# Sums for the means of values in three rounds over three tiles, the means put two tiles ahead, and all later keys reordered by GpSimd

## The chip, the cores and the metric

The kernel runs on one NeuronCore of a Trainium2 chip. The metric is the device time of one execution in microseconds (us). Engines are named as in the profile: PE is TensorE (PEld its weight loads), DVE is VectorE, ACT is ScalarE, POOL is GpSimd, and SP is the engine that issues most DMAs.

## The reference

Attention over 4 batches, 8 heads, 768 tokens and 64 numbers a head, in which each token sees its neighbours within 16 positions and, besides, one summary of every block of 32 tokens: the maximum of the block's keys and the mean of its values. The result feeds a mixture of 8 experts with one expert a token.

```python
k_sum = k.reshape(B, H, nb, block, D).max(axis=3)
v_sum = v.reshape(B, H, nb, block, D).mean(axis=3)          # the means of values: 24 a batch and head
scores_s = scale * einsum('bhsd,bhnd->bhsn', q, k_sum) + log(block)
a = softmax(concat([where(|i - j| < 16, scale * q @ k.T, -1e9), scores_s]))
attn = a @ concat([v, v_sum])                               # x, the experts' input, is attn by token
e_idx = argmax(x @ w_gate)                                  # one expert a token
out[e_idx == e] = gate * sigmoid(x @ w_output_gate)[e] * (relu(x @ w1[e]) @ w2[e])
```

## The kernel before

**Attention** works on 24 tiles of 128 tokens, six a batch, in a loop (L552) whose pass i is called tile i below; tiles 6, 12 and 18 begin batches 1, 2 and 3. The order of all instructions in it is written by hand. Pass i does, in this order:

- `scores(i + 2)` on PE (`sp`, L321) and the mask on DVE (`pr`, L326);
- `values` and `norm` of the tiles that are due, from tile 4 on tile i - 1 (`pv`, L364; `den`, `xs`, L374 to L378);
- `turn_p(i)`: PE turns the probabilities (`pt`, L353), ACT evacuates them (`pT`);
- `smallest(i + 2)` on DVE (`mn`, L333), then `exps(i + 1)` on ACT (`pr`, L342);
- the lists `early` and `put`: `gather_means` and `put_means`;
- now and then a reorder of queries on POOL, and the lists `rts` (routing) and `todo` (`prep_q`, `prep_k`, `means`);
- `subtract(i + 2)` on POOL (`pr`, L338), the store of `xs`, V loads on SP (L585 to L591), and reorders of keys: for batch 1 on POOL, for batches 2 and 3 on ACT (`nat_k`, L234), three each;
- turns of `xs` for the routing (`xtr`, L390).

**Means.** The windows of V of a batch lie in `VW`, 12 blocks of 64 rows. `means(b)` (L249) multiplies them with constant matrices: 12 matmuls into four 32-row strips of one PSUM bank (`ms`, L253), a 13th for the last 16 tokens (L255), and an ACT evacuation into `MT`. They run in one piece: in tile 2 for batch 0, and in tiles 5, 11 and 17 for batches 1, 2 and 3. `gather_means(b)` (L259) adds the two halves of each mean by a matmul (`mg`, L261) and evacuates them into `mst`; it runs in tiles 2, 6, 12 and 18. `put_means(t)` (L267) copies the 24 means into both of tile t's windows in `VW`, one on ACT and one on DVE; it runs one pass before the tile's `values`, so in pass t from tile 4 on, and for tiles 0 to 3 two at a time in passes 2 and 3.

**PSUM.** Four tags of two banks each ("TR", "S", "PT", "PV") are handed out in turn by `bank` (L215), so that every eighth allocation meets the same bank.

**Experts.** At the end of tile 18 SP begins to load weights (`raw`, L801). Which expert's weights these are comes from small DVE steps on the routing counts (`early_slots`, the last of them `esia`, L667, in tile 18), and the token lists that POOL fetches (`lst`, L763) wait for the list scatters (`l_dr`, L472). ACT and DVE split each weight tile in two (L809, L810) between the passes 19 to 23. After the last tile the experts' matmuls (`hp` L839 to L841, `yp` L933 to L935) keep PE busy to the end.

Of the kernel before, what the change touches and what calls it, by code (L numbers as in the profile page):

```python
# [21 lines left out]
P = 128  # L22
# [50 lines left out]
def constants():  # L73
# [21 lines left out]
    for m in range(3):  # L95
        c[r, C_AVG + 32 * m + 2 * m + (r + PAD) // 32] = 1.0 / 32.0
    c[LW + NS:LW + NS + PAD, C_AVG + 96 + 6] = 1.0 / 32.0
    for j in range(NS):
        c[32 * (j // 6) + 1 + j % 6, C_SUM + j] = 1.0
        if j % 6 == 5 and j < NS - 1:  # L100
            c[32 * (j // 6 + 1), C_SUM + j] = 1.0
    return c
# [89 lines left out]
def attention(tc, const, sa, sb, st, ps, dr, q, k, v, id_sb, c_sb, wg_sb, x_dr, l_dr, rt, late_work):  # L192
# [55 lines left out]

    def means(b):  # L249
        mp = bank([P, H * D], f"ms{b}")  # L250
        for m in range(3):
            for j in range(4):
                nc.tensor.matmul(mp[32 * j:32 * j + 32], lhsT=c_sb[0:LW, C_AVG + 32 * m:C_AVG + 32 * m + 32],  # L253
                                 rhs=VW[b % 2][0:LW, 3 * j + m, :, 0:D], start=m == 0, stop=m == 2 and j < 3)
        nc.tensor.matmul(mp[96:P], lhsT=c_sb[0:W, C_AVG + 96:C_AVG + P], rhs=VW[b % 2][:, NB - 1, :, 0:D],  # L255
                         start=False, stop=True)
        evac(MT.rearrange("p h d -> p (h d)"), mp)

# [11 lines left out]

    ms, km = {}, {}

# [253 lines left out]
    def later(i, work, when=todo):  # L526
        when.setdefault(i, []).append(work)
# [24 lines left out]
    for i, (b, tok) in enumerate(tiles):  # L552
# [166 lines left out]
class Experts:  # L719
# [3 lines left out]
    def __init__(self, tc, const, ps, w1, w2, id_sb, x_dr, l_dr, rt, out):  # L723
        self.tc, self.const, self.ps, self.w1, self.w2 = tc, const, ps, w1, w2
        self.id_sb, self.x_dr, self.l_dr, self.rt, self.out = id_sb, x_dr, l_dr, rt, out
        self.slots, self.expert, self.raw, self.lists = {}, {}, {}, {}

    def fixed(self, pool, name, n, shape, dt):
# [292 lines left out]
```

## Time and profile before

| | us |
|---|---|
| median of 3 runs (lowest, highest) | 553.32 (552.46, 553.39) |
| the profiled execution | 555.07 |
| its span, first to last instruction | 553.3 |
| busy PE, DVE, ACT, POOL in the span | 490.2, 382.3, 328.8, 238.5 |
| attention, from the first `sp` to the last `pv` | 16.7 to 194.6 |
| experts' matmuls without a pause | 221 to 481 |

A row of the time line reads: start (us), duration (us), engine, line, operation, output<-inputs, shapes, how many instructions it merges (x), and in brackets how long the engine sat idle before it and what ended that. A row of the windows reads: stretch, its length, busy us (and instructions) of PE, PEld, DVE, ACT and POOL, the granted PE clock (1.00 is full), the DMA share, and GB/s. Many matmuls of a row are two instructions each, so `sp` of one tile shows as x32.

### The profile page before, as it was taken

Reading aid. Unit: us, or ns where it says so; the run is one execution under the profiler, and the core shown is the slowest. Engines: PE = TensorE matmul, PEld = TensorE weight load, DVE = VectorE, ACT = ScalarE, POOL = GpSimd, SP = SyncE. Lnnn points to the kernel's source line nnn. Section 1 sums busy time; section 2 is a strip of 40 time slices with the busy share of each in tenths; the row PEclk is TensorE's granted clock in tenths of the full one; section 3 lists DMA queues with packets and bytes.
Section 4 is the critical chain, followed back from the end, with each engine's and each line's share of the span. In section 5 each row is a group of like instructions: output and inputs, shape, how many; then the busy total and the mean of one; then the engine's idle time right before and its main releaser. Section 6 shows DMA issues by size and latency. Waiting matters only on the chain.

```text
span 553.3 us, 12768 instructions
## 1 busy us (share of the span) xinstructions
PE 490.2 (89%) x4396; PEld 413.4 (75%) x4396; DVE 382.3 (69%) x822; ACT 328.8 (59%) x634; POOL 238.5 (43%) x268
## 2 busy tenths in 40 slices
PE   6686999898984887999999999999999999968880
PEld 6545677577563776889898998989989898846660
DVE  3748579989979776866666665575765757648891
ACT  4455597697565754555555655465654656537780
POOL 8755426358585551387453363434411203121110
PEclk9898999999998697999999999999999999989996
DMA  9998947867246478386856759576694664648860
GB/s 235 198 243 189 251 117 190 197 127 155 67 81 189 135 199 276 42 275 218 292 193 217 234 165 289 175 262 170 233 322 142 242 231 153 210 145 309 291 239 20
DMA packets 105810, 109.53 MB, mean 198 GB/s; under 512 B 43294, under 2 KB 68030, under 8 KB 105728
## 3 DMA queue, kind: packets, MB, share of 16 engines
q1 hardware_dynamic: 96208, 88.20, 54.9%
q0 software_dynamic: 9520, 20.33, 12.1%
q8 instruction: 39, 0.64, 0.5%
q14 instruction: 43, 0.35, 0.2%
HBM read 97.53 MB, written 13.59 MB: 201 GB/s over the span
## 4 chain that ended last, share of the span: by engine, by line
PE 57%; issue 12%; DMA 10%; DVE 9%; ACT 7%; POOL 2%; POOLq 0%; SPq 0%; DVEq 0%; ACTq 0%
PE yp L934 7%; PE yp L935 7%; PE hp L839 7%; PE yp L933 7%; PE hp L840 7%; PE hp L841 7%; DMA out_dram<-y,lst 5%; DMA raw<-in_moe_w_dram 3%; PE sp L321 3%; PE pv L364 3%; PE ms L253 2%; PE pt L353 2%; DVE pr L326 2%; DMA xg<-x_dr,lst_half 2%; PE xp L821 1%
## 5 line engine op out<-in xcount | busy, mean ns | idle before, releaser
L839 PE MATMUL hp<-xhl,w1h 128*128 128x256 f32 x384 | 109.7, 288 | 3.4 <-DVE hl L843 3.4
L840 PE MATMUL hp<-xhl,w1h 128*128 128x256 f32 x384 | 109.7, 286 | 0.0
L841 PE MATMUL hp<-xhl,w1l 128*128 128x256 f32 x384 | 109.5, 286 | 0.0
L809 ACT ACTIVATE w2h<-raw 128x512 fp32r<-128x512 f32 x104 | 63.8, 629 | 70.1 <-PE yp L935 31.4
L810 DVE TENSOR_TENSOR w2l<-raw,w2h 128x512 fp32r<-128x512 f32 x104 | 69.8, 686 | 42.1 <-ACT w2h L809 41.4
L933 PE MATMUL yp<-w2h,hh 128*128 128x512 f32 x216 | 86.5, 400 | 1.2 <-ACT hh L903 1.2
L935 PE MATMUL yp<-w2h,hl 128*128 128x512 f32 x216 | 84.9, 394 | 0.2
L934 PE MATMUL yp<-w2l,hh 128*128 128x512 f32 x216 | 85.0, 394 | 0.0
L776 POOL DMA_INDIRECT xg<-x_dr,lst x28 | 33.1, 1182 | 112.6 <-PE xp L821 100.6
L839 PEld LDWEIGHTS hp<-xhl,w1h 128*128 128x128 f32 x384 | 74.4, 194 | 5.1 <-DVE hl L843 3.6
L840 PEld LDWEIGHTS hp<-xhl,w1h 128*128 128x128 f32 x384 | 74.7, 195 | 0.9
L841 PEld LDWEIGHTS hp<-xhl,w1l 128*128 128x128 f32 x384 | 74.7, 195 | 0.0
L810 DVE TENSOR_TENSOR w1l<-raw,w1h 128x512 fp32r<-128x512 f32 x104 | 67.6, 703 | 8.8 <-ACT w1h L809 7.7
L843 DVE SCALAR_TENSOR_TENSOR hl<-hp,hh 128x256 fp32r<-128x256 f32 x96 | 39.3, 420 | 43.4 <-ACT hh L842 43.3
L842 ACT ACTIVATE hh<-hp 128x256 fp32r<-128x256 f32 x96 | 36.2, 379 | 52.6 <-PE hp L841 50.5
L338 POOL TENSOR_TENSOR pr<-pr,mn 128x960 f32<-128x960 f32 x24 | 45.1, 1881 | 49.2 <-DVE mn L333 26.7
L809 ACT ACTIVATE w1h<-raw 128x512 fp32r<-128x512 f32 x104 | 57.5, 620 | 5.8 <-DMA raw<-in_moe_w_dram 4.8
L933 PEld LDWEIGHTS yp<-w2h,hh 128*128 128x128 f32 x216 | 40.7, 189 | 10.0 <-ACT hh L903 2.1
L935 PEld LDWEIGHTS yp<-w2h,hl 128*128 128x128 f32 x216 | 40.6, 188 | 9.8 <-DVE hl L904 1.1
L211 ACT ACTIVATE pT<-pt 120x512 f32<-120x512 f32 x48 | 26.2, 594 | 34.0 <-PE pt L353 34.0
L934 PEld LDWEIGHTS yp<-w2l,hh 128*128 128x128 f32 x216 | 40.7, 188 | 7.6
L763 POOL DMA_INDIRECT lst<-l_dr,rowib x34 | 36.8, 1082 | 18.8 <-issue 9.5
(303 smaller groups left out, 901.1 us busy)
## 6 DMA issues: line engine op xcount, KB each, us to landing
raw<-in_moe_w_dram SPq DMA_DIRECT2D x208, 256.0 KB, 5.1
raw_k<-in_k_dram SPq DMA_DIRECT2D x12, 512.0 KB, 6.5
raw_q<-in_q_dram SPq DMA_DIRECT2D x12, 512.0 KB, 5.9
x_dr<-xs POOLq DMA_DIRECT2D x24, 256.0 KB, 3.2
vw<-in_v_dram SPq DMA_DIRECT2D x44, 128.0 KB, 4.7
vw<-in_v_dram SPq DMA_DIRECT2D x33, 64.0 KB, 4.4
vw<-in_v_dram POOLq DMA_DIRECT2D x11, 64.0 KB, 6.0
lst<-l_dr,rowib POOLq DMA_INDIRECT x34, 3.8
```

Source lines behind the costliest of these rows:

```text
L338: nc.gpsimd.tensor_tensor(pr, pr, mns.pop(i).unsqueeze(2).to_broadcast([P, H, W]), ALU.subtract)
L763: i = nc.gpsimd.indirect_dma_start(out=lst[:, t, :], out_offset=None, in_=self.l_dr, in_offset=bass.IndirectOffsetOnAxis(ap=self.slots[s][ ...
L809: nc.scalar.activation(hi, raw, AF.Copy)
L810: nc.vector.tensor_tensor(lo, raw, hi.bitcast(F32), ALU.subtract)
L839: nc.tensor.matmul(hp, lhsT=w_h[:, fs], rhs=self.xh[:, c, :], start=c == 0, stop=False)
L840: nc.tensor.matmul(hp, lhsT=w_h[:, fs], rhs=self.xl[:, c, :], start=False, stop=False)
L841: nc.tensor.matmul(hp, lhsT=w_l[:, fs], rhs=self.xh[:, c, :], start=False, stop=c == NC - 1)
L842: nc.scalar.activation(hh[:, j, :], hp, AF.Relu)
L843: nc.vector.scalar_tensor_tensor(hl[:, j, :], hp, 0.0, hh[:, j, :].bitcast(F32), ALU.max, ALU.subtract)
L933: nc.tensor.matmul(y, lhsT=hh[:, j, tk], rhs=w_h, start=j == 0, stop=False)
L934: nc.tensor.matmul(y, lhsT=hh[:, j, tk], rhs=w_l, start=False, stop=False)
L935: nc.tensor.matmul(y, lhsT=hl[:, j, tk], rhs=w_h, start=False, stop=j == NF - 1)
```

## The change

Five things change, all in attention.

1. `means(b)` is cut in three rounds, `means(b, m)`. Round m sums blocks 4m to 4m + 3 (before, strip j took blocks 3j to 3j + 2, so that each round needed the whole batch; the constants follow). The rounds of batch 0 stand in tiles 0, 1 and 2, those of batches 1 to 3 in the three tiles that end with 5, 11 and 17. The gather stays where it was.
2. The sum keeps a bank of its own over the three tiles: "TR" shrinks to one bank, a tag "MS" gets one, and `bank` now turns over seven banks. `take_x` of the experts takes "TR" and "MS" in turn.
3. `put_means(t)` runs one pass earlier, but not before the batch's gather: in pass 2 for tiles 0 to 3, in pass t - 1 for most, and for the first two tiles of batches 1 to 3 together in passes 6, 12 and 18.
4. `smallest(i + 2)` moves behind `exps(i + 1)` and behind the lists `early` and `put`, so DVE puts means first and reduces afterwards.
5. The six reorders of keys of batches 2 and 3 move from ACT to POOL.

```diff
-PB = {"S": 2, "PT": 2, "PV": 2, "TR": 2}
+PB = {"S": 2, "PT": 2, "PV": 2, "TR": 1, "MS": 1}
...
-    turn = itertools.cycle(("TR", "S", "PT", "PV"))
+    turn = itertools.cycle(("TR", "S", "PT", "PV", "S", "PT", "PV"))
...
-    def means(b):
-        mp = bank([P, H * D], f"ms{b}")
-        for m in range(3):
-            for j in range(4):
-                nc.tensor.matmul(mp[32 * j:32 * j + 32], lhsT=c_sb[0:LW, C_AVG + 32 * m:C_AVG + 32 * m + 32],
-                                 rhs=VW[b % 2][0:LW, 3 * j + m, :, 0:D], start=m == 0, stop=m == 2 and j < 3)
+    def means(b, m):
+        if m == 0:
+            mps[b] = ps.tile([P, H * D], F32, name=f"ms{b}", tag="MS", bufs=PB["MS"])
+        mp = mps[b]
+        for j in range(4):
+            nc.tensor.matmul(mp[32 * j:32 * j + 32], lhsT=c_sb[0:LW, C_AVG + 32 * m:C_AVG + 32 * m + 32],
+                             rhs=VW[b % 2][0:LW, 4 * m + j, :, 0:D], start=m == 0, stop=m == 2 and j < 3)
...
-        later(first - (1 if b == 0 else 2), lambda b=b: means(b), early if b == 0 else todo)
+        for m in range(3):
+            later(first - (3 if b == 0 else 4) + m, lambda b=b, m=m: means(b, m), early if b == 0 and m == 2 else todo)
         later(first - 1, lambda b=b: gather_means(b), early)
     for t in range(n):
-        later(live[t] - 1, lambda t=t: put_means(*tiles[t]), put)
+        first = live[t - t % TB]
+        later(max(live[t] - 2, first - 1), lambda t=t: put_means(*tiles[t]), put)
...
         turn_p(i)
-        if i + AHEAD < n:
-            smallest(i + AHEAD)
         if i + 1 < n:
             exps(i + 1)
         for x in early.pop(i, []) + put.pop(i, []):
             x()
+        if i + AHEAD < n:
+            smallest(i + AHEAD)
...
-                reorder("k", kb, u, "p" if kb == 1 else "a")
+                reorder("k", kb, u, "p")
...
-    def take_x(self, n, tag="TR"):
+    def take_x(self, n):
...
+            tag = next(self.turn)
```

In the order of the instructions, names carry batch and tile: `ms1` is the sum of batch 1, `sp12` belongs to tile 2 of batch 1, and the last number of a name is a buffer's. PE at the end of tile 5, before:

```order
L279 MATMUL qtr111_925<-id_sb_66,nat_q11_810 128x128 x4
L253 MATMUL ms1_931<-vw1_170,c_sb_68 32x512 x12
L255 MATMUL ms1_931<-vw1_170,c_sb_68 32x512
L390 MATMUL xtr04_956<-id_sb_66,xs04_882 128x128 x4
L321 MATMUL sp120_963<-kt1_168,qt0_165 64x120
```

The whole sum stands there in a row, ahead of the next tile's scores. PE at the end of tile 3 now, ahead of the scores of tile 6 (`sp10`), the first of batch 1:

```order
L283 MATMUL ktr121_689<-id_sb_66,nat_k12_562 128x128 x4
L256 MATMUL ms1_697<-vw1_170,c_sb_68 32x512 x4
L394 MATMUL xtr00_715<-id_sb_66,xs00_603 128x128 x4
L394 MATMUL xtr01_722<-id_sb_66,xs01_628 128x128 x4
L325 MATMUL sp100_728<-kt1_168,qt1_166 64x120
```

Four of the twelve matmuls have moved up to here; four more stand at the end of tile 4, and the last four with the 13th where all thirteen were.

DVE in tile 18, where the means of batch 3 (`mst3`) arrive, before (`mn32` is the minimum of tile 20, `esa` to `esia` the expert's index for the first weights):

```order
L378 TENSOR_TENSOR xs25_2387<-pv251_2378,den25_2388 128x256
L333 TENSOR_REDUCE mn32_2407<-pr32_2366 128x8
L209 COPY vw1_170<-mst3_2412 24x8x64
L209 COPY lg2_2181<-lt23_2418 128x32
L657 TENSOR_REDUCE esa_2436<-pasta_2333 128x3
L659 TENSOR_SCALAR nonea_2439<-esa_2436 128x3
L660 TENSOR_TENSOR rowa_2343<-rowa_2343,nonea_2439 128x3
L661 TENSOR_SCALAR rowia_2347<-rowa_2343 128x3
L662 TENSOR_SCALAR rowia_2347<-rowa_2343 128x3
L667 TENSOR_SCALAR esia_2437<-esa_2436 128x3
```

And now:

```order
L382 TENSOR_TENSOR xs25_2387<-pv251_2378,den25_2388 128x256
L211 COPY vw1_170<-mst3_2410 24x8x64 x2
L337 TENSOR_REDUCE mn32_2416<-pr32_2366 128x8
L211 COPY lg2_2188<-lt23_2420 128x32
L663 TENSOR_REDUCE esa_2438<-pasta_2333 128x3
L665 TENSOR_SCALAR nonea_2441<-esa_2438 128x3
L666 TENSOR_TENSOR rowa_2343<-rowa_2343,nonea_2441 128x3
L667 TENSOR_SCALAR rowia_2347<-rowa_2343 128x3
L668 TENSOR_SCALAR rowia_2347<-rowa_2343 128x3
L673 TENSOR_SCALAR esia_2439<-esa_2438 128x3
```

The minimum has moved behind two copies that wait for the gather; what follows it keeps its place. POOL in tiles 5 and 6, now (`nat_k20` and `nat_k21` are the first keys of batch 2; before, their two rows were not there, and the others stood in the same order):

```order
L342 TENSOR_TENSOR pr11_872<-pr11_872,mn11_914 128x960
L387 DMA x_dr_74<-xs04_893 128x512
L238 COPY nat_k20_952<-raw_k20_713 128x1024
L238 COPY nat_q12_1033<-raw_q12_536 128x1024
L342 TENSOR_TENSOR pr12_981<-pr12_981,mn12_1031 128x960
L387 DMA x_dr_74<-xs05_1002 128x512
L238 COPY nat_k21_1064<-raw_k21_839 128x1024
```

One copy of keys is added behind each of three subtractions and their stores, ahead of the next query reorder or subtraction.

More of the change, by code (lines that the diff above doesn't have):

```diff
@@ L95, in constants @@
     for m in range(3):
[L96 to L101, printed above, removed]
+        c[r, C_AVG + 32 * m + 3 * m + (r + PAD) // 32] = 1.0 / 32.0
+    c[LW + NS:LW + NS + PAD, C_AVG + 96 + 9] = 1.0 / 32.0
+    for blk in range(NB):
+        at = 32 * (blk % 4) + 3 * (blk // 4)
+        c[at + 1, C_SUM + 2 * blk] = c[at + 2, C_SUM + 2 * blk + 1] = 1.0
+        if blk:
+            c[at, C_SUM + 2 * blk - 1] = 1.0
+    c[96 + 9, C_SUM + NS - 1] = 1.0
     return c
@@ L247, in load_vw @@
                 (engine or nc.sync).dma_start(t[p0:p0 + m, :, 0:D], v[b, :, s0 + r0:s0 + r0 + m, :].rearrange("h s d -> s h d"))
[L249 to L257 removed]
+    def means(b, m):
[5 more added lines that the diff above has]
+                             rhs=VW[b % 2][0:LW, 4 * m + j, :, 0:D], start=m == 0, stop=m == 2 and j < 3)
+        if m == 2:
+            nc.tensor.matmul(mp[96:P], lhsT=c_sb[0:W, C_AVG + 96:C_AVG + P], rhs=VW[b % 2][:, NB - 1, :, 0:D],
+                             start=False, stop=True)
+            evac(MT.rearrange("p h d -> p (h d)"), mp)
     def gather_means(b):
@@ L726, in __init__ @@
         self.slots, self.expert, self.raw, self.lists = {}, {}, {}, {}
+        self.turn = itertools.cycle(("TR", "MS"))
     def fixed(self, pool, name, n, shape, dt):
```

2 lines of the change are left out of this document (1 added, 1 removed).

## The prediction

> **What bounds the kernel now.** I read the windows first, to see which engine is full in which stage.
>
> ```profile
> 65.00:78.00 13.00, 13.00 (x192) 8.15 (x190) 6.89 (x15) 9.83 (x19) 5.75 (x5) 1.00 0.77 210
> 91.00:104.00 13.00, 9.72 (x176) 8.03 (x176) 12.38 (x29) 7.70 (x15) 6.78 (x8) 1.00 0.89 217
> 234.00:247.00 13.00, 13.00 (x88) 11.92 (x87) 8.56 (x23) 8.18 (x18) 9.74 (x8) 1.00 0.74 232
> ```
>
> The limit changes from tile to tile. Tiles 5 and 6 (65 to 78) fill PE; tiles 9 and 10 (91 to 104), where DVE does the routing as well, fill DVE with 12.38 of 13 us and leave PE 3.3 us idle. From 221 on the experts fill PE without a pause, and nothing of that stage is edited. So the change is worth what it takes off the way to the first expert's matmuls. The chain of waits tells what that way is at its end.
>
> ```profile
> 160.09 5.86 DMA raw<-in_moe_w_dram
> ...
> 198.09 12.49 DMA raw<-in_moe_w_dram
> ...
> 212.49 0.58 PE hp L839
> ```
>
> The weight stream starts at 160 and paces the rest, but it starts only when DVE has computed the expert's index in tile 18. So attention up to tile 18 is on the path, and a shift there reaches the end.
>
> **Tiles 2 to 4: the means of batch 0 and the copies of means.** First the time line of DVE, of POOL and of ACT.
>
> ```profile
> 38.20 3.15 DVE L209 COPY vw<-mst 24x512 f32<-24x512 f32 x2 [4.56 <-ACT mst L211]
> 47.33 2.35 DVE L209 COPY vw<-mst 24x512 f32<-24x512 f32 x2
> 49.71 2.48 DVE L293 TENSOR_REDUCE km<-ktr 128x16 f32<-128x512 f32 x4
> 93.10 0.42 DVE L209 COPY vw<-mst 24x512 f32<-24x512 f32 x1
> ```
>
> ```profile
> 38.10 1.04 POOL L236 COPY nat_q<-raw_q 128x1024 f32<-128x1024 f32 x1 [4.43 <-DMA raw_q<-in_q_dram]
> 39.11 1.96 POOL L338 TENSOR_TENSOR pr<-pr,mn 128x960 f32<-128x960 f32 x1
> 47.45 1.95 POOL L338 TENSOR_TENSOR pr<-pr,mn 128x960 f32<-128x960 f32 x1 [4.22 <-DVE mn L333]
> 51.66 1.53 POOL L300 COPY kt<-km 128x288 f32<-128x288 f32 x4 [2.26 <-DVE km L293]
> ```
>
> ```profile
> 47.45 2.33 ACT L211 ACTIVATE kt<-ktr 128x384 f32<-128x384 f32 x8
> ```
>
> A copy of means takes 0.42 us alone, but two of them took 3.15 and 2.35 us, and they ended (41.35, 49.68) with the POOL work that ran beside them (41.07, 49.40): DVE stood until POOL was through. DVE has no pause from 38.20 to 52.2, then `k_sum` (L300) follows, and it releases the scores of batch 1. After the change the copies stand ahead of the minimum, so the subtraction can't be running beside them. The gather also comes earlier; here is PE.
>
> ```profile
> 32.05 2.78 PE L253 MATMUL ms<-vw,c_sb 64*32 64x512 f32 x24
> 34.76 1.04 PE L255 MATMUL ms<-vw,c_sb 120*32 120x512 f32 x2
> 52.14 1.88 PE L321 MATMUL sp<-kt,qt 64*64 64x120 f32 x32 [4.14 <-POOL kt L300]
> 53.94 3.73 PE L364 MATMUL pv<-vw,pT 120*64 120x65 f32 x64
> 60.34 1.05 PE L321 MATMUL sp<-kt,qt 64*64 64x120 f32 x32
> 61.32 1.15 PE L364 MATMUL pv<-vw,pT 120*64 120x65 f32 x32
> ```
>
> A sum costs 2.71 + 0.99 = 3.7 us of PE (from start to start), a round 2.71 / 3 = 0.9. With two rounds gone to tiles 0 and 1, where PE waits anyway, 1.9 us is left in tile 2 and the gather comes 1.8 us sooner, or less if the last V blocks land late; I take 1.5. On DVE, four copies in tile 2 and one in tile 3 cost 5 x 0.42 = 2.1 in place of 5.5. That makes 1.5 + 3.4 = 4.9 for DVE alone. But the maxima (`km`) are released by ACT's evacuations (`kt`, 47.45 to 49.78), and ACT wins less: about 2.2 through PE (the 1.5 of the gather, and `values` that no longer wait for the 3.15 us), and 0.6 for one copy fewer in tile 3, so 2.8. Term 1: **-3.0** (bounds -1.5 and -4.9).
>
> **The PE clock in tile 4.** While PE waits 4.14 us for the keys of batch 1, its clock falls: `sp` takes 1.88 in place of 1.05 and two tiles of `pv` 3.73 in place of 2 x 1.15, 2.26 us too much on a PE that is then the bound (with the turns behind it, 2.4). Here are the windows there and behind another pause, and the rows of two shorter pauses.
>
> ```profile
> 51.00:54.00 3.00, 1.86 (x34) 1.47 (x34) 1.19 (x2) 0.00 (x0) 2.34 (x6) 0.51 0.58 128
> 171.00:174.00 3.00, 3.00 (x47) 2.58 (x40) 2.88 (x8) 0.92 (x2) 1.13 (x2) 0.51 0.44 158
> ```
>
> ```profile
> 93.81 1.13 PE L321 MATMUL sp<-kt,qt 64*64 64x120 f32 x32 [1.30 <-ACT qt L211]
> 169.44 0.68 PE L390 MATMUL xtr<-id_sb,xs 128*128 128x128 f32 x4 [3.11 <-DVE xs L378]
> ```
>
> After the change a round of 0.9 stands in this pause, PE's `xtr` come about 2.2 sooner and the keys 3.0: the pause is 4.14 - 0.9 - (3.0 - 2.2), about 2.5 us. The clock fell after 3.11 us and not after 1.30; 2.5 lies between and nearer to 3.11. Both ends stay in the range, 0 and -2.4. I take full clock, but barely: 3.11 is a pause in which almost nothing ran, while the round cuts this one's idle in two. Term 2: **-2.4**.
>
> [...]
>
> **Batch 1, tiles 3 to 8.** Of its sum, round 0 falls into the pause above, round 1 costs 0.9 in tile 4, and tile 5, where PE is full, loses 1.8: net -0.9. From tile 6 ACT is nearly as full as PE. It loses three reorders, but gets the second copy of the first two tiles, and the wait of the gather still runs through it; that gives back about 0.6.
>
> ```profile
> L234 ACT ACTIVATE nat_k<-raw_k 128x1024 f32<-128x1024 f32 x7 | 7.4, 1061 | 0.1
> L236 POOL COPY nat_k<-raw_k 128x1024 f32<-128x1024 f32 x4 | 4.3, 1086 | 2.3 <-DMA raw_k<-in_k_dram 2.2
> ```
>
> A reorder takes the same on both engines. POOL is busy 5.75 of 13 us in tiles 5 and 6, and the copy stands behind the subtraction and the store, with a pass to spare before PE turns the keys; what it is moved past is the list scatters and the next query reorder, which have as much slack. I cost it at nothing; without that cover it is 1.06 us a copy. Term 3: **-0.3** (bounds +0.6 and -1.8).
>
> **Batches 2 and 3, tiles 9 to 18.** PE loses 1.8 us in tile 11 and in tile 17 and gets 0.9 in tiles 9, 10, 15 and 16, where it waits (1.30 us in tile 9). But there DVE is the bound, and it loses a cover:
>
> ```profile
> 93.79 1.45 DVE L425 TENSOR_TENSOR d<-lg,mx 128x48 f32<-128x48 f32 x1
> ```
>
> ```profile
> 93.25 1.92 POOL L338 TENSOR_TENSOR pr<-pr,mn 128x960 f32<-128x960 f32 x1 [1.40 <-ACT ls L211]
> 155.12 1.80 POOL L338 TENSOR_TENSOR pr<-pr,mn 128x960 f32<-128x960 f32 x1
> 169.86 1.00 POOL L763 DMA_INDIRECT lst<-l_dr,rowia  x1 [4.94 <-DMA l_dr<-pair,posi]
> ```
>
> The routing step at 93.79 stood behind the subtraction, and the 0.42 us copy before it (93.10) lay in that shadow. Now the copy comes ahead of the minimum: +0.42 in each of tiles 9, 10, 15 and 16. In tile 18 it matters most:
>
> ```profile
> 153.71 1.14 DVE L333 TENSOR_REDUCE mn<-pr 128x8 f32<-128x960 f32 x1
> 155.24 1.97 DVE L209 COPY vw<-mst 24x512 f32<-24x512 f32 x1 [0.38 <-ACT mst L211]
> 158.22 0.16 DVE L667 TENSOR_SCALAR esia<-esa 128x3 int32<-128x3 f32 x1
> ```
>
> Before, the minimum was done at 154.85 and the copy waited out the subtraction, until 157.2; `esia` followed at 158.2. Now the minimum waits for the gather and two copies. With the gather 1.7 sooner (153.5, after PE's 1.8), the copies end about 155.3 beside a query reorder, the minimum 156.45, the subtraction 158.4; then the small steps behind it, stalled as at 93.79, bring `esia` to about 159.1. So the weight index comes 0.8 later against the DVE of its batch, and the three scatters behind that subtraction, for which the token lists wait (169.86), 1.5. Against that, batch 2 wins about 1.1 by tile 14, its own two copies taken off, since tile 12 waits less for tile 11's sum. Sum: -1.1 for batch 2, +0.84 for the copies of tiles 15 and 16, +1.2 (between 0.8 and 1.5) for tile 18, near +1.0. Term 4: **+1.0** (bounds -1.5 and +2.5).
>
> **Tiles 21 to 23.** Putting two tiles ahead takes a wait away here:
>
> ```profile
> 178.00 1.00 ACT L342 ACTIVATE pr<-pr 128x960 f32<-128x960 f32 x1 [2.59 <-POOL pr L338]
> ```
>
> ```profile
> 179.69 0.51 PE L364 MATMUL pv<-vw,pT 120*64 120x65 f32 x10 [3.81 <-ACT vw L211]
> ```
>
> `values` of tile 21 waited for a copy queued on ACT behind the exponentials at 178.00. It now runs before them; the turn behind it, which had to wait until 179.69 + 1.1 = 180.8, starts when the exponentials end, at about 179.0. ACT's own queue hides part of that. Term 5: **-1.0** (bounds 0 and -3, the latter if the clock stays up there too).
>
> The bank turn is shorter by one, so that a query turn meets the bank of the scores of the same tile one allocation sooner; DVE has evacuated them by then in all but the routing tiles. I cost it inside term 4. The experts' `take_x` has two banks as before.
>
> **Sum.** -3.0 - 2.4 - 0.3 + 1.0 - 1.0 = -5.7 us on the profiled execution of 555.07 us:
>
> ```profile
> core 0: 553.3 us, clock 0.959
> ```
>
> The span is 553.3, and 1.8 us lie around it. The median of the runs is 553.32; the shift carries over to it: 553.3 - 5.7 = **547.6 us**. A measurement of this kernel can tell some 0.2%, 1.1 us, from no change.
>
> **Rivals.**
>
> *A, the clock still falls in tile 4.* For it: the pause of 3.11 us. Against it: the pause is cut by a round. Term 2 is then gone: 547.6 + 2.4 = **550.0 us**. Chance 0.30.
>
> *B, slower: the minimum behind the gather becomes the bound in tiles 6, 12 and 18.* In tile 18 the subtraction ran from 155.12; behind the gather (155.2 on the old times), two copies, and the minimum it would run from 157.4, 2.3 us later. It decides once the subtraction ends later than ACT is ready for the exponentials of that tile, one pass on. If no slack were left, three tiles at 2.3 us each cost 6.9: 547.6 + 6.9 = **554.5 us**. Against it: a pass lasts 5 us or more, and ACT's queue is full in tiles 7 and 13. Chance 0.09.
>
> *C, POOL's six copies of keys block DVE.* A POOL copy of queries runs 1.04 us at 38.10 beside a stalled DVE copy. If each new copy meets such a DVE step, 6 x 1.09 = 6.5 us are lost: 547.6 + 6.5 = **554.1 us**. Against it: in tiles 5 to 8, 12 and 13 DVE's only such steps are the copies of means; the 24 minima, the longest DVE steps there, are all but constant whatever POOL does:
>
> ```profile
> L333 DVE TENSOR_REDUCE mn<-pr 128x8 f32<-128x960 f32 x24 | 27.5, 1145 | 0.2
> ```
>
> Their mean of 1145 ns is that of the single one at 153.71. Chance 0.07.
>
> [...]
>
> **How the numbers follow.** Forecast 0.50, A 0.30, B 0.09, C 0.07; 0.04 are left for what I don't see. Each of B and C may come in part: about half of their chance ends below 552.2 still. Faster by over 0.2%: 0.50 + 0.30 + 0.05 = 0.85. Within 0.2%: 0.07. Slower: 0.08. The range goes from 543.4 (terms 1, 3 and 5 each at the better half of their bounds: 0.9 + 0.8 + 1.0, and 1.5 of term 4) to 552.2 (A, with term 1 at its low bound and 0.7 of term 4): 543.4 to 552.2.
>
> **What would show it.** In the profile after: the DVE copies of means at 0.42 us apiece in tile 2; `sp` of tile 6 about 3 us sooner than 52.14 and 1.05 us long (1.88 by A); tile 5's `ms` 1.9 us; the first weight load about 5 us sooner than 160; `hp` without a pause from about 215. Term 1 is wrong if a round of `ms` waits for V; B shows as ACT's exponentials waiting for POOL in tiles 7, 13 and 19; C as DVE copies that end with `nat_k`. If the weight stream starts 5 us sooner and the experts don't, the path was not what I take it for.

## The result, and the profile after

The changed kernel takes 555.65 us (median of 20 runs, 552.12 to 559.91) where the kernel before took 553.83 beside it: a ratio of 1.006, with a 95% interval of 1.0038 to 1.0082. It is slower by 0.6%. The ratio and its interval, here and below, compare executions of the two kernels that were not in a slower state of the chip, so it is not the quotient of the two medians (1.003). The forecast was 547.6, and the range ended at 552.2. The profiled execution has a span of 555.2 us at a mean granted clock of 0.945 (before: 553.3 and 0.959).

I read the profile after in the order of the prediction's steps. First the windows that stood at its head.

```profile
65.00:78.00 13.00, 13.00 (x194) 9.03 (x187) 7.86 (x21) 9.34 (x19) 6.83 (x7) 1.00 0.82 198
91.00:104.00 13.00, 11.29 (x182) 8.21 (x182) 12.44 (x31) 5.63 (x12) 5.66 (x5) 0.87 0.96 221
234.00:247.00 13.00, 13.00 (x101) 12.60 (x100) 8.45 (x32) 5.32 (x13) 7.17 (x7) 1.00 0.39 130
```

The limits are the same ones: PE in tiles 5 and 6 and in the experts, DVE (12.44 of 13) in tiles 9 and 10. New is the clock of 0.87 in the second row. Next PE in tiles 0 to 4.

```profile
24.85 1.09 PE L357 MATMUL pt<-id_sb,pr 128*120 128x128 f32 x8 [2.60 <-ACT pr L346]
25.88 1.86 PE L256 MATMUL ms<-vw,c_sb 64*32 64x512 f32 x8
27.67 1.88 PE L325 MATMUL sp<-kt,qt 64*64 64x120 f32 x32
...
52.29 1.54 PE L325 MATMUL sp<-kt,qt 64*64 64x120 f32 x32 [0.99 <-POOL kt L304]
53.77 2.09 PE L368 MATMUL pv<-vw,pT 120*64 120x65 f32 x64
```

Two things happen at once. The pause ahead of tile 6's scores is 0.99 us in place of 4.14 and the clock stays up there, as forecast. But the clock falls elsewhere (0.50 from 26.0 to 32.8 us): after a pause of 2.60 us, in which PE waits for tile 0's exponentials, the first round of the sum takes 1.86 us in place of the 1.06 that later rounds take, the scores 1.88 in place of 1.05. Tile 2's exponentials start 8.17 us behind tile 0's (31.97 and 23.80), where it was 5.65 before (28.43 and 22.78): 2.5 us lost. This profile also begins 1.0 us later, with tile 0's exponentials at 23.80 in place of 22.78. So tile 6's scores start at 52.29, where they started at 52.14. (`sp` takes 1.54 us there although the granted clock is 1.00 from 52 to 54 us; the forecast for full clock was 1.05.) Now DVE in tiles 2 and 18.

```profile
40.41 1.42 DVE L211 COPY vw<-mst 24x512 f32<-24x512 f32 x4 [4.04 <-ACT mst L213]
...
153.40 1.62 DVE L211 COPY vw<-mst 24x512 f32<-24x512 f32 x2 [0.37 <-ACT mst L213]
155.04 1.15 DVE L337 TENSOR_REDUCE mn<-pr 128x8 f32<-128x960 f32 x1
156.41 1.75 DVE L665 TENSOR_SCALAR nonea<-esa 128x3 f32<-128x3 f32 x1
...
158.53 0.16 DVE L673 TENSOR_SCALAR esia<-esa 128x3 int32<-128x3 f32 x1
```

Four copies in tile 2 take 1.42 us, with GpSimd idle beside them (0.00 us busy from 40 to 42 us). In tile 18 the minimum stands behind the copies, and a step of the index (`nonea`) ends at 158.16, with the subtraction beside it (156.34 to 158.12). GpSimd shows what follows.

```profile
156.34 1.78 POOL L342 TENSOR_TENSOR pr<-pr,mn 128x960 f32<-128x960 f32 x1 [1.95 <-DVE lg L211]
...
161.55 1.06 POOL L476 DMA_INDIRECT l_dr<-pair,posi  x1 [0.19 <-issue]
...
172.49 1.00 POOL L770 DMA_INDIRECT lst<-l_dr,rowia  x1 [6.62 <-DMA l_dr<-pair,posi]
...
178.37 1.00 POOL L783 DMA_INDIRECT xg<-x_dr,lst  x1 [1.72 <-DVE mx L427]
179.40 1.80 POOL L342 TENSOR_TENSOR pr<-pr,mn 128x960 f32<-128x960 f32 x1
```

The subtraction of tile 20 waits 1.95 us, until its minimum (155.04 to 156.19) and the small copy `lg` behind it are done; the three scatters of list entries stand behind it, and the last is issued at 161.55. The list's fetch then waits until 172.49 for them to land (before: 169.86). The subtraction of tile 22 stands behind that fetch, and behind the fetch of x (`xg`) by that list, on GpSimd's queue. (The last wait of `xg` is put down to `mx`, a DVE step of the routing. It does not need that step: in e14 below it runs at 171.69, and `mx` at 175.89.) ACT waits for the subtraction:

```profile
181.22 1.00 ACT L346 ACTIVATE pr<-pr 128x960 f32<-128x960 f32 x1 [3.91 <-POOL pr L342]
```

That was 178.00 and 2.59 us. The chain of waits shows where this ends.

```profile
161.59 5.93 DMA raw<-in_moe_w_dram
...
179.40 1.81 POOL pr L342
...
203.28 12.33 DMA raw<-in_moe_w_dram
...
217.51 0.58 PE hp L847
```

The last of these was at 212.49. So the trace suggests two theories. **Theory 1, order:** the minimum behind the copies makes the list late in tile 18, and this costs more than all that is won. **Theory 2, clock and banks:** the rounds and the shorter turn of banks let PE's clock fall in tiles 0 to 2, 10 and 16 (0.50 from 26.0 to 32.8, from 97.7 to 101.1 and from 138.7 to 142.1 us).

### The profile page after: what moved, and what is told of

Same layout as the page of the kernel before. It is cut to its first block, busy times and chain, and to the rows that moved or that the text cites. A ratio compares the mean times of both kernels' runs of the same rounds, so it can differ in the third digit from the quotient of the medians.

```text
span 555.2 us, 12743 instructions
## 1 busy us (share of the span) xinstructions
PE 497.9 (90%) x4396; PEld 415.6 (75%) x4396; DVE 381.5 (69%) x822; ACT 323.7 (58%) x628; POOL 239.3 (43%) x274
## 4 chain that ended last, share of the span: by engine, by line
PE 58%; issue 12%; DMA 11%; DVE 9%; ACT 5%; POOL 4%; SPq 0%; POOLq 0%; DVEq 0%; ACTq 0%
PE yp L942 7%; PE yp L943 7%; PE yp L941 7%; PE hp L847 7%; PE hp L849 6%; PE hp L848 6%; DMA out_dram<-y,lst 5%; PE sp L325 4%; DMA raw<-in_moe_w_dram 3%; PE pv L368 3%; PE pt L357 3%; DMA xg<-x_dr,lst_half 2%; PE ms L256 2%; PE xtr L394 2%; DVE pr L330 1%
## 5 line engine op out<-in xcount | busy, mean ns | idle before, releaser
L342 POOL TENSOR_TENSOR pr<-pr,mn 128x960 f32<-128x960 f32 x24 | 43.0, 1790 | 52.4 <-DVE lg L211 15.7
L964 POOL DMA_INDIRECT out_dram<-y,lst x24 | 26.4, 1102 | 34.6 <-DVE y L961 30.6
```

Of the source, the lines that this page charges most:

```text
L342: nc.gpsimd.tensor_tensor(pr, pr, mns.pop(i).unsqueeze(2).to_broadcast([P, H, W]), ALU.subtract)
```

## The experiments

The ratio of each run is to the kernel before, measured beside it on the same chip. On two occasions (e1 to e4, and e9 to e12) PE also waits inside the experts' matmuls, for nothing that the profile names:

```profile
L941 PE MATMUL yp<-w2h,hh 128*128 128x512 f32 x160 | 63.9, 399 | 1.2 <-issue 1.2
```

This is a group of e1 from 230 to 480 us; the kernel before has 0.0 us there in its own profile. The six groups of e1 wait 6.2 us in all, so this is only a part of the difference: on those occasions the kernel before took 570.08 and 567.15 us. It was not the chip as such: on the chip of e1 to e4 the kernel before took 552.42 us later, beside e16 and e17. From these runs I take the marks up to 180 us, and their ratios only with care.

### One part undone: e1 to e4

**e1**, the minimum ahead again:

```
         turn_p(i)
+        if i + AHEAD < n:
+            smallest(i + AHEAD)
...
             x()
-        if i + AHEAD < n:
-            smallest(i + AHEAD)
```

> The changed kernel (555.65 us) with one part undone: the minimum stands again ahead of the exponentials, the gather and the copies of means. Theory 1, order: the minimum behind the gather and two copies delays the subtraction of tile 20 in pass 18, the scatters behind it, the list's fetch (172.49 in the profile after, 169.86 before) and so the expert's first x; undoing it gives the list back: 552.5 us (0.998 of before), the list's fetch near 170. Theory 2, clock and banks: the loss comes from PE's half clock in tiles 0 to 2, 10 and 16 and from the shorter bank turn; the minimum's place is worth nothing there: 555 us (1.003), scores of tile 6 still near 52.3. My own prediction counted 5 passes with the minimum later as a cost of about 1 us in pass 18: by it 554.5.

Measured: 571.35 us, ratio 0.999 (0.9948 to 1.0032). The list's fetch comes 8.97 us after the index (166.97 and 158.00), where it took 13.96 after the change. Theory 1's mark came; the ratio decides nothing.

**e2**, means put one tile ahead: `later(live[t] - 1, ...)`.

> The changed kernel with one part undone: means are put one tile ahead, as before, the minimum stays behind them. Theory 1, order: one copy fewer in front of the minimum in pass 18 (and in passes 6 and 12), the list's fetch 0.5 to 1 us sooner, but the values of tile 21 wait again for a copy queued on ACT: 555 us (1.002 to 1.004). Theory 2, clock and banks: no part of it is touched: 555.6 us. The term 5 of the prediction (1.0 us won by the second tile ahead in tiles 21 to 23): 556.5 us (1.005 or more).

Measured: 575.16 us, the kernel before 570.08; no interval. The list's fetch is at 170.12, 13.76 us behind the index: one copy fewer does not mend it. But tile 6's exponentials start at 60.06, where they started at 63.25 in the profile after: the half clock of tiles 0 to 2 is not there (`sp` takes 1.05 us at 27.01).

**e3**, keys of batches 2 and 3 on ACT: `reorder("k", kb, u, "p" if kb == 1 else "a")`.

> The changed kernel with one part undone: the keys of batches 2 and 3 are reordered on ACT again. Rival C of the prediction (POOL's copies of keys stop DVE): 6.5 us back at most, by the stalls seen at 107.4 (1.7 us behind the copy at 107.6) about 1.5 us: 554.0 us. Theory 1 and theory 2: 555.6 us, or up to 1 us slower, since ACT is nearly full from tile 6 on and loses 6 x 1.06 us.

Measured: 575.45 us, ratio 1.009 (1.0055 to 1.0125). Nothing comes back by this ratio; tile 13's exponentials start at 108.69, those of e2 (with the copies on GpSimd) at 109.07. One small DVE step does end with such a copy in the profile after (107.40 to 108.69, `nat_k` 107.61 to 108.66), but POOL's copies are not what costs, which e8 below says too. Rival C falls.

**e4**, the sums in one piece in the common turn:

```
-PB = {"S": 2, "PT": 2, "PV": 2, "TR": 1, "MS": 1}
+PB = {"S": 2, "PT": 2, "PV": 2, "TR": 2}
...
-        for m in range(3):
-            later(first - (3 if b == 0 else 4) + m, ...)
+        later(first - (1 if b == 0 else 2), lambda b=b: [means(b, m) for m in range(3)], ...)
```

> The changed kernel with one part undone: the sums for the means stand in one piece at their old place, in a bank of the common turn of eight, as before; the order of the minimum, the puts two ahead and the keys on GpSimd stay. Theory 2, clock and banks: PE keeps full clock in tiles 0 to 2, 10 and 16 and no longer waits for the scores' bank: 552.5 us (0.998), scores of tile 6 near 50 (52.29 after, 52.14 before). Theory 1, order: the list stays late: 555.5 us or more, the list's fetch at 172 or later. The prediction's terms: 1.8 us lost in tile 2 and a pause of about 4 us with a half clock in tile 4 back: 558 us.

Measured: 568.64 us, ratio 0.9953 (0.9914 to 0.9993). By itself this speaks for theory 2. But PE's clock is half from 53.0 to 56.4 us in its profile, behind a pause of 2.22 us in tile 4 (two tiles of `pv` take 3.64 us, 2.09 in the profile after), its list is as late as that of the change (13.56 us behind the index), and e5, e6 and e16 below speak against it at undisturbed times. I leave this ratio unexplained.

### One part alone: e5 to e8

The four were run together, undisturbed, where the kernel before took 552.74 us.

**e5**, the rounds with their bank; minimum, puts and keys as before (the edits of e1, e2 and e3 together, made on the changed kernel).

> The kernel before with one part of the change alone: the sums in three rounds over three tiles with their own bank (and so a turn of seven banks); the minimum, the puts and the keys as before. Theory 2, clock and banks: the mean granted clock falls by about 0.004 against before (0.949 against 0.953), which at half speed is 2 x 0.004 x 553 = 4.4 us of halved windows, worth 1 to 2 us at the end: 1.002 to 1.004 of before. Theory 1, order: nothing delays the list; with the rounds' gain in tiles 2 to 4 (3 us) this is 0.997 of before, list's fetch at or before 168.

Measured: 551.49 us, ratio 0.9974 (0.9938 to 1.0009), mean granted clock 0.959 against 0.958. The clock is not lower, so theory 2's price isn't there. PE in tile 4:

```profile
49.49 1.54 PE L325 MATMUL sp<-kt,qt 64*64 64x120 f32 x32 [2.56 <-POOL kt L304]
50.96 3.52 PE L368 MATMUL pv<-vw,pT 120*64 120x65 f32 x64
```

The rounds alone bring tile 6's scores 2.65 us sooner, but leave a pause of 2.56 us and the clock falls behind it (`pv` takes 3.52 us, 2.09 in the profile after).

**e6**, the minimum behind the puts, in the kernel before:

```
-        if i + AHEAD < n:
-            smallest(i + AHEAD)
         if i + 1 < n:
             exps(i + 1)
         for x in early.pop(i, []) + put.pop(i, []):
             x()
+        if i + AHEAD < n:
+            smallest(i + AHEAD)
```

> The kernel before with one part of the change alone: the minimum behind the exponentials, the gather and the copies of means. Theory 1, order: from the expert's index (esia) to the start of the list's fetch it takes about 13.5 us in place of the 9 to 11.6 of the kernels with the minimum ahead, and the time is 1.004 to 1.006 of before. Theory 2: equal to before within 0.1%, the copies in tile 2 are unlocked and give 1 to 3 us there, which comes to 0.997 at best.

Measured: 555.71 us, ratio 1.0041 (1.0009 to 1.0074), as theory 1 has it. GpSimd in tile 18:

```profile
158.29 1.79 POOL L342 TENSOR_TENSOR pr<-pr,mn 128x960 f32<-128x960 f32 x1 [1.62 <-DVE lg L211]
...
163.50 1.06 POOL L476 DMA_INDIRECT l_dr<-pair,posi  x1 [0.19 <-issue]
...
175.26 1.22 POOL L768 DMA_INDIRECT lst<-l_dr,rowia  x1 [7.42 <-DMA l_dr<-pair,posi]
```

The wait for the minimum and the late list (14.79 us behind the index at 160.47) come from this one edit.

**e7**, the sums in one piece, in a bank of their own (the turn of seven):

```
+    turn = itertools.cycle(("TR", "S", "PT", "PV", "S", "PT", "PV"))
...
+            mps[b] = ps.tile([P, H * D], F32, name=f"ms{b}", tag="MS", bufs=PB["MS"])
```

> The kernel before with one part of the change alone: the sums in one piece, but in a bank of their own, so that the turn has seven banks in place of eight. If the shorter turn is what hurts (PE's waits for the scores' bank of 0.3 to 2.2 us in tiles 9, 10, 15, 16 and 18 after the change): 1.002 to 1.004 of before, clock about 0.949. If it is the rounds' place that lets the clock fall: 1.000, clock 0.953 as before, with PE's waits of tiles 9 and 10 there all the same. Theory 1: 1.000.

Measured: 554.85 us, ratio 1.0031 (1.0004 to 1.0059). The waits on the scores' bank in the routing tiles are there:

```profile
98.67 0.29 PE L453 MATMUL tot<-ohb,ones 128*128 128x8 bf16 x6 [0.61 <-DVE pr L330]
99.24 0.62 PE L411 MATMUL lt<-c_sb,ls 128*128 128x16 f32 x4 [0.27 <-DVE pr L330]
```

The kernel before has a wait of 0.46 us at the second place and none at the first. The shorter turn costs something, at the edge of what can be told; the rounds (e5) more than pay for it.

**e8**, puts two ahead and keys on GpSimd, sums in one piece, minimum ahead.

```
+        first = live[t - t % TB]
+        later(max(live[t] - 2, first - 1), lambda t=t: put_means(*tiles[t]), put)
...
+                reorder("k", kb, u, "p")
```

> The kernel before with two parts of the change alone: means put two tiles ahead, keys of batches 2 and 3 reordered on GpSimd; the sums in one piece in the common turn, the minimum ahead. Theory 1 and theory 2 both take the loss of the change out: the prediction's term 5 (1 us in tiles 21 to 23) and three reorders less on ACT in tiles 6 to 8 remain: 0.997 to 0.999 of before, near 552 us, clock as before. If the puts or POOL's copies are what costs (rival C): 1.002 or more.

Measured: 553.08 us, ratio 1.0008 (0.9979 to 1.0038). Neither gain nor loss: between what the theories and what rival C forecast, and without the loss of the change.

### The whole change, and eight banks: e9 to e12

**e9** is the changed kernel again. **e10** has the minimum ahead from pass 18 on:

```
+        if i + AHEAD < n and i >= 18:
+            smallest(i + AHEAD)
         if i + 1 < n:
             exps(i + 1)
...
-        if i + AHEAD < n:
+        if i + AHEAD < n and i < 18:
             smallest(i + AHEAD)
```

**e11** gives the sums' bank back to the turn while no sum is open, and **e12** does both:

```
+    turn = itertools.cycle(("TR", "S", "PT", "PV", "MS", "S", "PT", "PV"))
...
+        if tag == "MS" and summing:
+            tag = next(turn)
```

> The changed kernel itself, to stand beside the next ones on one chip. Singly, the rounds with their bank gave 0.9974 of before, the minimum 1.0041, the puts and keys 1.0008, which together is 1.0023 (554 us); the first measurement gave 1.006. Theory 1: between 1.002 and 1.006, the list's fetch 13 to 14 us behind the expert's index. [...]

> The changed kernel, but from pass 18 on (tiles 20 to 23) the minimum stands ahead of the exponentials again, as before the change; up to pass 17 it stays behind the copies. Theory 1, order, says that these four places alone cost: the time from the index to the list's fetch falls from 13 or 14 us to 9 to 11.5 and the loss turns: 0.994 to 0.997 of before, near 550.5 us. If the minimum costs in passes 2 to 17 as well (tiles 8 and 14, whose subtractions end 8.06 us after the scores' first add in place of 5.38): 1.000 to 1.002. If the order isn't it: as the changed kernel on this chip.

> The changed kernel, but the bank of the sums takes part in the turn (eight banks) while no sum is open. Theory of the banks (the seven-bank turn alone cost 1.0031): PE's wait of 2.19 us for the query turn in tile 18 goes, the one in tiles 9, 10, 15 and 16 stays, since a sum is open there; 0.999 of the changed kernel, since the list is late all the same (553 us beside 554). If banks were the main loss: 0.997 of it, equal to before. Theory 1: as the changed kernel within 0.1%.

> Both of the last two: the minimum ahead from pass 18 on, and the sums' bank in the turn while no sum is open. Theory 1 with the banks' part: 0.992 to 0.996 of before, near 549.5 us, and faster than the minimum's place alone by 0.1 to 0.2%. If both theories are wrong: as the changed kernel on this chip.

Measured: e9 573.6 us, ratio 0.9963 (0.9891 to 1.0035); e10 568.91, 1.0028 (0.9988 to 1.0068); e11 576.34, 1.0157 (1.0108 to 1.0205); e12 575.95, 1.0149 (1.0095 to 1.0202). By these ratios e10 is not faster than e9, against theory 1, and e11 and e12 are slowest. The runs were disturbed, and I read no price from them; what e11's edit is worth stays open. The marks: e10 has its list at 163.68, 9.06 us behind the index (e9: 174.30, 13.93 us). The eight banks (e11) bring the list no sooner (176.06); with the minimum ahead as well (e12) it is at 167.17. e9 shows the half clock in tiles 0 to 2 a second time, after a pause of 3.14 us (`sp` takes 1.88 us at 28.00). But e1, e2, e3 and e5 have the same rounds and keep the clock there (`sp` takes 1.05 us), so the rounds alone don't bring it.

### The cures: e13 to e17

e13 is e10 again, undisturbed. **e14** leaves the minimum late, but issues pass 18's scatters ahead of the subtraction; **e15** makes this edit alone in the kernel before; **e16** has the edits of e13 and e14; **e17** is the changed kernel beside e16.

```
+        for x in scat.pop(i, []) if i == 18 else []:
+            x()
         if i + AHEAD < n:
             subtract(i + AHEAD)
```

> The changed kernel with the minimum ahead of the exponentials from pass 18 on, a second time, since the experts' stage was disturbed on the chip of the first. Theory 1 (the list): 0.993 to 0.997 of before, near 550 us; the list's fetch within 9 us of the index (9.06 in the first run), the exponentials of tile 22 near 175 to 177 in place of 181.22. Theory 2 (clock and banks): 1.002 to 1.006, as the change.

> The changed kernel, but in pass 18 the three scatters of list entries stand ahead of GpSimd's subtraction (tile 20), which still waits for the late minimum. Theory 1, by the way of the landing: the last scatter is issued before the weight stream starts (about 157 in place of 161.55, the stream starts at 159.7), lands in 2 to 6 us in place of 9.9, the list's fetch comes at 163 to 167 in place of 172.49, and the subtraction of tile 22 no longer waits; but the subtraction of tile 20 ends about 2 us later and the exponentials of tile 20 with it: 0.996 to 1.000 of before, so 0.6 to 1% under the change. If the loss sits in the late subtraction itself (attention, not the list): 1.008 or more. Theory 2: 1.006.

> The kernel before with this one edit: in pass 18 the three scatters stand ahead of the subtraction of tile 20. By the landing: issued at 155 to 158 in place of 157.75 to 161.27, ahead of the weight stream (159.4), the list's fetch at 163 to 166 in place of 169.86, the subtraction of tile 22 up to 4 us sooner; tile 20's subtraction 3.9 us later, its exponentials up to 0.7 us: 0.996 to 0.999 of before. If the list's time is hidden behind the weights anyway: 1.000 to 1.003.

> The changed kernel with the minimum ahead of the exponentials from pass 18 on and, in pass 18, the scatters ahead of the subtraction. If both cures take away one loss (the list that comes late), they don't add: 0.989 to 0.993 of before, near 549 us, the list's fetch at 161 to 164.5. If the late subtraction costs by itself, beside the list: 1 us or more under either cure, 0.987 to 0.990. If the earlier cures were luck of the chip: 1.000 or more.

> The changed kernel itself, beside the cured form. Theory 1: 1.002 to 1.006 of before and 1.0 to 1.6% over the cured form; list's fetch 13 to 14 us behind the index, last scatter issued 1.8 us behind the first weight load. If the cures were luck of the chip: within 0.3% of the cured form.

All runs that were undisturbed, with marks from one profile each. The kernel before took 552.74 us beside e5 to e8, 553.07 beside e13 to e15 and 552.42 beside e16 and e17. "Lag" is the issue of the last scatter less that of the first weight load, "landing" the end of that issue to the start of the list's fetch, in us. In e14 the fetch did not wait for the landing, so its 8.6 is only an upper bound:

| kernel | time, us | ratio (95%) | lag | landing | list's fetch | span |
|---|---|---|---|---|---|---|
| before | 553.83 | | 0.8 | 8.6 | 169.86 | 553.3 |
| after | 555.65 | 1.006 (1.0038 to 1.0082) | 1.8 | 9.9 | 172.49 | 555.2 |
| e5 rounds alone | 551.49 | 0.9974 (0.9938 to 1.0009) | 0.8 | 8.3 | 167.34 | 551.4 |
| e6 minimum alone | 555.71 | 1.0041 (1.0009 to 1.0074) | 1.7 | 10.7 | 175.26 | 555.6 |
| e7 bank alone | 554.85 | 1.0031 (1.0004 to 1.0059) | 0.8 | 7.8 | 170.44 | 552.2 |
| e8 puts and keys | 553.08 | 1.0008 (0.9979 to 1.0038) | 0.5 | 6.5 | 170.56 | 551.9 |
| e13 minimum ahead late | 548.92 | 0.9892 (0.9851 to 0.9932) | 0.5 | 6.6 | 164.64 | 550.0 |
| e14 scatters ahead | 549.43 | 0.9929 (0.9896 to 0.9962) | -1.4 | under 8.6 | 164.76 | 550.1 |
| e15 before, scatters ahead | 550.03 | 0.9884 (0.9837 to 0.9931) | -0.1 | 7.3 | 165.36 | 550.5 |
| e16 both cures | 549.55 | 0.9939 (0.9905 to 0.9974) | -0.2 | 6.9 | 163.96 | 546.8 |
| e17 after again | 555.73 | 1.0057 (1.0026 to 1.0088) | 1.8 | 10.6 | 169.60 | 552.4 |

GpSimd in e13:

```profile
151.71 1.79 POOL L342 TENSOR_TENSOR pr<-pr,mn 128x960 f32<-128x960 f32 x1
...
157.13 0.96 POOL L476 DMA_INDIRECT l_dr<-pair,posi  x1 [0.19 <-issue]
...
164.64 1.00 POOL L772 DMA_INDIRECT lst<-l_dr,rowia  x1 [2.89 <-DMA l_dr<-pair,posi]
...
172.33 1.80 POOL L342 TENSOR_TENSOR pr<-pr,mn 128x960 f32<-128x960 f32 x1
```

and in e14, where the same subtraction comes still later than in the change (6.40 us behind tile 19's exponentials, where it was 4.59) but no longer in front of the scatters:

```profile
155.25 0.96 POOL L476 DMA_INDIRECT l_dr<-pair,posi  x1 [0.19 <-issue]
156.23 1.80 POOL L342 TENSOR_TENSOR pr<-pr,mn 128x960 f32<-128x960 f32 x1
...
164.76 1.23 POOL L772 DMA_INDIRECT lst<-l_dr,rowia  x1 [0.30 <-issue]
```

Both take the list back to about 164.7 and the time to 0.99 of before, and e13 to e15 all gained more than I had expected. Since e14 is as fast, the loss is not in the late subtraction itself. e16 shows that the cures don't add up: it comes to 0.9939, just above its expected 0.989 to 0.993, and no better than either alone; they mend one loss. The changed kernel beside it came as expected: 555.73 against 549.55 us on one chip, 1.1% (its list lies 14.68 us behind the index, where I had expected 13 to 14). So the place of the minimum from pass 18 on is what makes the change a loss, by the scatters that it delays in pass 18. In e13 and e14 the first weight load comes no sooner than in e17 (156.64, 156.62 and 156.19), so the list is what they gain by. In e15 it also comes 2.3 us sooner than before (157.22 and 159.50), so there the gain is not the list's alone.

e17 is the telling trace, since its clock stayed up in tiles 0 to 2 (1.00 from 20.2 to 27.0 us). First PE in tile 4, then ACT, GpSimd and the minimum of tile 22 on DVE behind tile 18:

```profile
48.74 1.55 PE L325 MATMUL sp<-kt,qt 64*64 64x120 f32 x32 [0.99 <-POOL kt L304]
50.22 2.09 PE L368 MATMUL pv<-vw,pT 120*64 120x65 f32 x64
```

```profile
154.56 1.00 ACT L346 ACTIVATE pr<-pr 128x960 f32<-128x960 f32 x1 [0.53 <-POOL pr L342]
...
162.12 0.63 ACT L816 ACTIVATE w1h<-raw 128x512 fp32r<-128x512 f32 x1 [2.86 <-DMA raw<-in_moe_w_dram]
164.12 0.63 ACT L816 ACTIVATE w1h<-raw 128x512 fp32r<-128x512 f32 x1 [1.37 <-DMA raw<-in_moe_w_dram]
...
165.62 1.00 ACT L346 ACTIVATE pr<-pr 128x960 f32<-128x960 f32 x1
...
178.46 1.00 ACT L346 ACTIVATE pr<-pr 128x960 f32<-128x960 f32 x1 [3.71 <-POOL pr L342]
```

```profile
157.96 1.05 POOL L476 DMA_INDIRECT l_dr<-pair,posi  x1 [0.19 <-issue]
...
169.60 1.01 POOL L770 DMA_INDIRECT lst<-l_dr,rowia  x1 [7.32 <-DMA l_dr<-pair,posi]
...
176.62 1.80 POOL L342 TENSOR_TENSOR pr<-pr,mn 128x960 f32<-128x960 f32 x1
```

```profile
168.23 1.15 DVE L337 TENSOR_REDUCE mn<-pr 128x8 f32<-128x960 f32 x1
```

The same places before:

```profile
160.13 1.00 ACT L342 ACTIVATE pr<-pr 128x960 f32<-128x960 f32 x1
167.46 1.00 ACT L342 ACTIVATE pr<-pr 128x960 f32<-128x960 f32 x1
```

```profile
160.32 0.95 POOL L472 DMA_INDIRECT l_dr<-pair,posi  x1 [0.19 <-issue]
```

Tile 20's exponentials start at 154.56, 5.57 us sooner than before (160.13). Tile 22's start at 178.46, 0.46 us later than before (178.00). The whole gain of the attention is waited away in between: first 3.7 us for the weights, whose splits stand in ACT's queue ahead of tile 21's exponentials (165.62, 1.84 us sooner than before), then 2.3 us for the list. Tile 22's minimum was done at 169.38, 7.2 us before its subtraction. In all eleven kernels of the table this subtraction starts within 0.05 us of the end of the second fetch of x, with its minimum done 3.3 to 8.0 us earlier. So that fetch, and the list behind it, sets tile 22 in every one of them, the mended ones too. Over the eleven spans of the table, the correlation with the list's fetch is 0.92, with tile 20's exponentials 0.09; these are single profiles of kernels that share edits. The mean clock of e17's runs is 0.950, that of the kernel before beside it 0.958, and that of e16, which has the same rounds and the same turn of seven banks, 0.957. So the lower clock goes with the late list and not with the rounds, and theory 2 falls as the account of the loss.

## Why the prediction was wrong

**Terms 1 and 2** (tiles 2 to 4, -3.0 and -2.4) held in size. From the exponentials of tile 0 to those of tile 6, before took 41.42 us and e17 takes 36.61: 4.8 us won for 5.4 forecast. The four copies of tile 2 take 1.42 us (before, two took 3.15), and PE keeps its clock in tile 4 (two tiles of `pv` take 2.09 us, 3.73 before). `sp` won less there than forecast, 1.55 us in place of 1.05, so that `sp` and `pv` together took 1.97 us less than before, for 2.26 forecast. I had this last point by the wrong pause: I expected 2.5 us and took it as short enough; the pause came out at 0.99, and 2.56 (e5) let the clock fall. So the right call on this clock was in part luck. Rival A doesn't hold.

What I had not priced is the start. In the profile after and in e9, PE's clock is half in tiles 0 to 2 behind a pause of 2.60 and 3.14 us for the first exponentials, where the first round of the sum now stands, and only 2.0 us are left by tile 6. In e17, the same code, the pause is 1.88 us and the clock stays. Theory 2 made the rounds the cause; e7 and e8, without rounds, show the same fall (at 26.2 and 25.7 us; `sp` takes 1.88 us behind it in both).

**Terms 3 and 4 up to tile 17** held as a sum; their parts were not told apart. At tile 19's exponentials e17 is 5.45 us ahead of before (148.14 and 153.59), or 5.76 from the exponentials of tile 0; terms 1 to 3, with -1.1 and +0.84 of term 4, made 5.96. In the profile after it was only 2.86 from tile 0's exponentials, by the half clock at the start.

**The step that failed is tile 18 in term 4**: "the weight index comes 0.8 later [...], and the three scatters behind that subtraction, for which the token lists wait (169.86), 1.5", priced at 1.2. The edit, the place and the sign were right, and the size was off. In e17 the index is 3.30 us ahead of before where the attention was 5.45 ahead: 2.15 lost, for 0.8. The last scatter is issued 2.36 ahead (157.96 and 160.32): 3.1 lost, for 1.5. The list's fetch is 0.26 ahead: 5.2 lost. So two things were missing. The scatters come later by twice what was forecast, and then they also land 2.0 us later: in the table, 9.9 to 10.7 us after the last issue when it is 1.7 to 1.8 us behind the first weight load, and 6.5 to 8.6 us in the other kernels. And the prediction let the path go to the end through the weight stream alone ("a shift there reaches the end"); the list reaches it as well, because GpSimd's queue holds the fetch of the list and of x ahead of tile 22's subtraction. The sign that the prediction set for a wrong path came: in e17 the first weight load is issued 3.3 us sooner than before (156.19 and 159.50), and the `hp` that stood at 212.49 in the chain of waits comes 2.45 later (214.94; e13, e14 and e15 have it at 209.60, 209.75 and 209.38). With the list's place mended, e13 and e14 come to 548.92 and 549.43 us, inside the range, but not by the prediction's terms, as e15 shows; with it as it is, e17 is at 1.0057.

That the landing grows with the weight loads issued ahead of the scatters is an estimate of mine from the lag in the seventeen traces in which the fetch waited for the landing (6.1 to 6.6 us at a lag of 0.5, 7.8 to 8.6 at 0.8, 8.9 to 11.5 at 1.7 to 1.8). But ahead of the first load (e15, e16) it was 7.3 and 6.9, no shorter than at 0.5, and a kernel that holds the weights back was not run. So no run shows what lengthens the landing.

**Term 5** (-1.0) came in its place, but nearly nothing of it reached the end. The turn behind tile 22's exponentials starts 1.05 us after their start in e17 and 1.06 in e8 (before 2.77), so the wait for the copy is gone. But tile 23's exponentials follow tile 22's by 4.92 and 4.95 us in place of 5.26, so only 0.3 us is won there, and e8, which has the second tile ahead, is at 1.0008.

**Rival B** named the edit and tile 18, but gave it too little: it looked at ACT's exponentials one pass on. In e17 those of tile 20 wait 0.53 us. The scatters behind the subtraction were the way. **Rival C** fell with e3.

What stays open: the ratio of e4, and by how much the shorter turn of banks costs inside the whole change (e11 was disturbed). Also, e17's loss of 0.57% is that of its twelve runs (551.94 to 558.51); the span of its one profile is 0.9 us shorter than that of the kernel before, so the trace shows how the gain is lost, and not the size of the loss. And e15, with nothing of the change, is as fast as e13, e14 and e16: once the list comes early, the 4 to 5 us that the attention gains show no further gain that these intervals can tell. The fetch of x still holds tile 22 in all four.

## What to carry to other kernels

When an edit delays one instruction on an engine, list what stands behind it in each queue, and follow each to its own consumer; the one that starts a transfer needs a price for its landing among the traffic of that moment (6.5 to 10.7 us in the table), not only for its start. A gain in one stage is worth only what the next hand-over passes on: here that was the arrival of a list, and moving three scatters ahead of one subtraction in the kernel before (e15) was worth as much as the whole change with its list mended. Before trusting a profile on small things, take a second one of the same kernel: the half clock of tiles 0 to 2 was in two of three.

## What the runs showed of the hardware

In the first tiles PE's clock fell behind long pauses for the first exponentials: 2.35 (e8), 2.47 (e7), 2.60 (after) and 3.14 us (e9). It stayed up at 26 us behind pauses of 1.44 to 2.23 us in all others. The length of a pause alone doesn't decide, though: in tile 4 the clock fell behind 2.21 (e8) and 2.22 us (e4). Here are windows of 3.4 us in the profile after and then in e17; the columns are those of the windows above, PE first and the clock third from the end.

```profile
22.60:26.00 3.40, 1.15 (x12) 0.98 (x16) 3.33 (x5) 1.46 (x2) 2.88 (x2) 1.00 1.21 179
26.00:29.40 3.40, 3.40 (x40) 1.53 (x36) 0.52 (x1) 1.52 (x3) 2.80 (x3) 0.50 0.63 120
```

```profile
20.20:23.60 3.40, 2.07 (x66) 1.66 (x65) 3.04 (x4) 1.31 (x3) 1.97 (x2) 1.00 1.22 233
23.60:27.00 3.40, 2.85 (x48) 1.82 (x48) 2.59 (x4) 2.47 (x4) 3.01 (x3) 1.00 1.01 151
```

A window in which PE was busy for 1.15 of 3.40 us was followed by half clock, one with 2.07 us was not. The steps of the clock lie 3.41 us or a multiple of it apart in each trace (26.0 and 32.8 in the profile after; 51.1 and 57.9 in that of the kernel before), so all nineteen traces can be cut into windows at their own steps. From 20 to 64 us, all 12 windows at full clock in which PE was busy for at most 1.76 us were followed by half clock, and none of the 217 with 1.78 us or more (before: 0.34 us, from 47.7 on, was followed by half clock; 1.80 us, from 20.4 on, was not). From 64 to 200 us it is less clean: below 1.70 us all were followed by half clock, between 1.70 and 2.82 us some were and some were not (after: 2.81 us, from 135.2 on, was; 1.85 us, from 155.7 on, was not). These are counts from the traces of this case alone, and what decides between 1.70 and 2.82 us they don't show.
